# Feed-forward weights staged slice by slice in one kept tile, and a sixth token-group of seven-product down projections, in a fused attention and GEGLU block

## The chip, the cores and the metric

The kernel runs on one core of a Trainium2 chip. Its time is device microseconds (us) of one launch. Before the change three runs took 998.12, 999.64 and 999.91 us, a median of 999.64 us. The engines are named as in the profile: PE is the matmul engine and PEld its weight loads, DVE is VectorE, ACT is ScalarE, POOL is GpSimd, and SP issues most of the DMAs.

## The reference

One pre-layernorm transformer block over 2048 tokens of width 640, in float32:

```
h  = x + softmax_windowed(q k^T * 20^-0.5) v @ wo      with q, k, v = layernorm(x) @ wqkv
h2 = h + (gelu(n @ w_gate) * (n @ w_up)) @ w_down      with n = layernorm(h)
```

There are 32 heads of 20 columns; each token sees itself and the 255 before it. The feed-forward part has 1536 inner columns and gelu in its tanh form. Layernorm has no learned scale.

## The kernel before, in words

**Precision.** A float32 matrix is split into two float16 parts, a high part and a low part (the rest after rounding). A product of two such matrices takes three float16 matmuls: high by high, high by low, low by high.

**Feed-forward work.** The tokens are cut into four chunks of 512 (c = 0 to 3), the inner columns into three groups of 512 (fg = 0 to 2). A pair (c, fg) is a group of work; `ORDER` (line 1132) lists the twelve of them: (0,0) (1,0) (0,1) (0,2) (1,1) (1,2), then chunks 2 and 3. For each group the gate and up projections come first. The first three groups use three plain products (`gate_up`, line 1175). The other nine (`PLAIN` = 3) are done in four `Quad`s each (line 1210), one for each 128 inner columns; a Quad uses sums and differences of the weights (`weight_sums`, line 1602, tile `ws`) and of the tokens (`token_sums`, line 1577, tiles `ts0`, `ts`, `wst`) to need fewer matmuls.

**Down projections.** After a group's four Quads its down projection runs, cut into pieces that are slipped between the steps of the next Quads (`fill`, line 1789). The plain form `down` (line 1343) does, for each of four blocks of 128 tokens and two halves of 320 columns, three products of four matmuls, 96 matmuls of 320 columns, and adds each result into the token tile `ht` with one DVE instruction straight from PSUM (8 for a group). The high-by-high, low-by-high and high-by-low products of two blocks and two halves are twelve matrix products for a pair of blocks. `down7` (line 1432) does the eight correction products among them by a scheme of seven, so eleven products of four matmuls for a pair of blocks, 88 matmuls for a group. It has the 8 additions from PSUM too, and beside them 8 results that ACT copies into four small tiles z (`to_z`, line 1458) and DVE adds to `ht`. It also needs four sums of the weights for each group (`seven_weights`, line 1383: two on POOL, two on DVE) and four sums of the tokens for each pair of blocks (`seven_tokens`, line 1411: two on POOL, two on DVE). `SEVEN` is the list of groups that take this form, `ORDER[FIRST7:-1]`.

**Names in the trace.** All instructions have line 199, so they are read by tile. w4 to w6 are the gate weights of the groups fg = 0 to 2, w7 to w9 the up weights, w10 to w12 the down weights, each with h or l for its part. The tile `ts` written from w10, w11 or w12 holds the weight sums of `down7`; its four z tiles lie in the room of w8l, the token sums in that of w9l. `wst` is the staging tile into which the raw float32 weights are loaded. `rr` and `gelt` take the sums that ACT copies out of a Quad's PSUM bank, `gel` the gated result, `ah` and `al` its two parts.

**Loading of weights.** `load_lane` (line 1641) brings the weights on the SP queue. wo and the first gate and up weights go through a ring of small tiles. The other seven (down 0, then gate, up, down of 1 and of 2) each go as a whole into `wst`: all its slices, of 512 columns five times for gate and up and of 640 columns four times for down, are issued together once the weight before it is `ready`, that is, once all slices of that one have been split. After that DVE takes the largest magnitude of each slice (`scale`, line 390), one small matmul spreads it over the partitions, and the split follows: ACT writes the high part of each slice, then the low part is made, for the first two slices by ACT and POOL and for the others by DVE (`split`, `low`).

**Order.** A planner writes all instructions out in one order. `Clock` (line 54) keeps a modelled time for each engine; each strand of work is a generator (a lane) that yields the engine it wants and the modelled time at which its inputs are there. In every turn the first lane in a list of priorities whose engine is free enough and whose inputs are there is stepped. Once the feed-forward part has the chip to itself, `FFBACK` (line 302) says how far an engine may be ahead for a lane to be let in: 0.75 us for what follows matmuls directly, 0.2 for the norms and the two lanes of sums, 0.1 for `token_sums`. On the chip each engine runs its instructions in that order, and waits by semaphores.

The norm of chunk 2 runs beside the group (1,1), the norm of chunk 3 beside (2,0); `token_sums(2)` is held until the last down weight is split, and takes a new tile with the name `wst`. The strand `seven_weights` starts once four Quads are done and the low parts of w8 and w9 are no longer needed.

Of the kernel before, what the change touches and what calls it, by code (L numbers as in the profile page):

```python
# [22 lines left out]
P = 128  # L23
# [230 lines left out]
def block_kernel(ctx: ExitStack, tc: tile.TileContext, x, wqkv, wo, wg, wu, wd, out):  # L254
# [57 lines left out]
    def need(*reads, slots=(), when=None, eng="tensor"):  # L312

        def f():
            if when and not when() or any(opened[n] >= banks[n] for n in slots):
                return INF
            return max([nc.ready(reads, eng)]
                       + [nc.slot(psums[n], n, banks[n]) for n in slots])
        return f
# [4 lines left out]
    def on(eng, *reads, when=None, after=None):  # L324
        f = need(*reads, when=when, eng=eng)
        if after is not None:
            return (eng,), lambda: max(f(), nc.others(after, eng))
        return (eng,), f
# [25 lines left out]
    class Weight:  # L354
# [5 lines left out]

        def __init__(self, src, shape, col, e=WE):
            self.src, self.shape, self.col, self.e = src, shape, col, e
            self.have = set()
            self.raw = {}

        @property
        def ready(self):
            return len(self.have) == self.shape[0]

        def load(self, room):  # L370
            for i in range(self.shape[0]):
# [16 lines left out]
            pos["used"] += self.sliced  # L388

        def scale(self, lane, tp="tp"):  # L390
            n = self.shape[0]
            am = nc.tile(lnp, [P, 8], F32, "am" + lane, 2 if lane == "0" else 1)
            nc.vector.memset(am[:, n:n + 1], _pow2(-100))
            for i in range(n):
                if self.hl and self.col != C_K:

                    yield on("scalar", self.raw[0, i])
                    nc.scalar.activation(self.hl[0][:, i, :], self.raw[0, i], AF.Abs,
                                         accum_out=am[:, i:i + 1])
                    continue  # L400
                yield on("vector", when=lambda: (0, i) in self.raw)
                yield on("vector", self.raw[0, i])
                nc.vector.tensor_reduce(am[:, i:i + 1], self.raw[0, i], axis=AX.X, op=ALU.max,
                                        apply_absolute_value=True)
                self.done_with()
            yield on("vector", am)
            nc.vector.tensor_reduce(am[:, 7:8], am[:, 0:n + 1], axis=AX.X, op=ALU.max)

            yield on("vector", am)
            nc.vector.tensor_scalar(am[:, 7:8], am[:, 7:8], _pow2(-self.e), None, op0=ALU.mult)  # L410
            hold = SETTLE if ffpools[1] else 0.0
            bound = need(am, slots=[tp])
            yield ("tensor",), lambda: bound() + hold
            t = bank(tp)
            nc.tensor.matmul(t[:, 0:P], am[:, 7:8].to_broadcast([P, P]), ident, start=True,
                             stop=True)
            pc = pw[:, self.col:self.col + 1]
            sc = sw[:, self.col:self.col + 1]
            yield soon("vector", t)
            nc.vector.tensor_reduce(am[:, 6:7], t[:, 0:P], axis=AX.X, op=ALU.max)  # L420
            done(tp)
            yield on("vector", am)
            nc.vector.tensor_scalar(pc.bitcast(I32), am[:, 6:7].bitcast(I32), 0x7F800000, None,
                                    op0=ALU.bitwise_and)
            yield on("vector", pc)
            nc.vector.tensor_scalar(sc.bitcast(I32), pc.bitcast(I32), -1, 0x7F000000,
                                    op0=ALU.mult, op1=ALU.add)
            self.scaled = True
            yield on("vector", pc)
            nc.vector.tensor_scalar(pc, pc, _pow2(self.e), None, op0=ALU.mult)  # L430
            self.known = True
# [6 lines left out]
        def split(self, pool, spread=0):  # L438
            self.room(pool)
            self.begun = True  # L440
            sc = sw[:, self.col:self.col + 1]
            for i in range(self.shape[0]):
                yield on("scalar", when=lambda: (1, i) in self.raw)
                yield on("scalar", sc, self.raw[1, i])
                nc.scalar.activation(self.hl[0][:, i, :], self.raw[1, i], AF.Copy, scale=sc)
                tasks.append(self.low(i, sc, i < spread))

        def low(self, i, sc, spread):
            hi, lo = (t[:, i, :] for t in self.hl)
            w = self.raw[1, i]  # L450
            if spread:
                yield on("scalar", w)
                nc.scalar.activation(w, w, AF.Copy, scale=sc)
                yield on("gpsimd", w)
                nc.gpsimd.tensor_tensor(lo, w, hi, op=ALU.subtract)
            else:
                yield on("vector", hi)
                nc.vector.scalar_tensor_tensor(lo, w, sc, hi, op0=ALU.mult, op1=ALU.subtract)
            self.have.add(i)
            self.done_with()  # L460
# [670 lines left out]
    NCH = S // (CB * P)  # L1131
    ORDER = [(0, 0), (1, 0), (0, 1), (0, 2), (1, 1), (1, 2)]
    ORDER += [(c, fg) for c in range(2, NCH) for fg in range(FG)]
    PLAIN, FIRST7 = 3, 6
    hts, ga = {}, {}
    ffpools = [None, None]

# [434 lines left out]
        if chunk[c] == CB:  # L1572
            side.append((LATE, token_sums(c)))

    TS, sums = {}, {}

    def token_sums(c):
        hh, hl = hT[c]
        h1, h2 = hh[:, :, :CW], hh[:, :, CW:]
        l1, l2 = hl[:, :, :CW], hl[:, :, CW:]  # L1580
        yield on("vector", when=lambda: ffpools[1] and (c < 2 or W["d", FG - 1].ready))
        t = (nc.tile(ffp, [P, KC, 512], F32, "ts" if c else "ts0") if c % 2 or not c else
             nc.tile(ffpools[0], [P, KC, 512], F32, "wst")).bitcast(F16)
        t = t.rearrange("p c (a n) -> p a c n", a=4)
        for ks in (slice(k, k + 1) for k in range(KC)):
            a, b, m, d = (t[:, i, ks] for i in range(4))
            yield on("vector", h1, h2)
            nc.vector.tensor_tensor(a, h2[:, ks], h1[:, ks], op=ALU.subtract)
            yield on("vector", a, l2)
            nc.vector.scalar_tensor_tensor(b, a, -_pow2(-TE), l2[:, ks], op0=ALU.mult, op1=ALU.add)  # L1590
            yield on("vector", b, l1)
            nc.vector.tensor_tensor(d, l1[:, ks], b, op=ALU.subtract)
            yield on("vector", l2, h2)
            nc.vector.scalar_tensor_tensor(m, l2[:, ks], _pow2(TE), h2[:, ks], op0=ALU.mult,
                                           op1=ALU.subtract)
        TS[c] = t
# [44 lines left out]
    def load_lane():  # L1641
        for w in weights[NW:NW + 3]:
            for turn in range(2):
                yield from w.load_slices(turn)
        rest = weights[NW + 3:]
        for i, w in enumerate(rest):
            yield ("sync",), need(when=lambda: ffpools[0] and (i < 1 or rest[i - 1].ready),
                                  eng="sync")
            t = nc.tile(ffpools[0], [P] + w.shape, F32, "wst")
            w.load([t[:, k, :] for k in range(w.shape[0])])  # L1650

    def scale_lane(todo, lane):
        for i in todo:
            w = weights[i]
            before = {2: W["k"]}.get(i)
            yield on("vector", when=lambda: (w.loaded or w.sliced) and (not before or before.scaled)
                     and (i < NW or B[0].maxima == H) and (i <= NW or B[0].scored))
            yield from w.scale(lane, "ra" if i < NW else "tp")
            if i == 0:
                yield on("vector", sw)  # L1660
                nc.vector.tensor_scalar(qs, sw[:, C_Q:C_Q + 1], _pow2(QE), None, op0=ALU.mult)
                pos["qs"] = 1
            if i == 1:
                yield on("vector", when=lambda: W["q"].known)
                qk_scale()
            if i == 2:
                yield on("vector", sw)
                nc.vector.tensor_scalar(vs, sw[:, C_V:C_V + 1], _pow2(VE), None, op0=ALU.mult)
                pos["vs"] = 1
            if i == NW:  # L1670
                yield on("vector", when=lambda: W["v"].known)
                wo_scale()
            if i > NW:
                kind, fg = later[i - NW - 1]
                if kind == "u":
                    ff_scales(fg)
                    pos["ffk", fg] = 1
                if kind == "d":
                    ff_scales_down(fg)
                    w.down = True  # L1680
# [292 lines left out]
```

## Time and profile before

| | |
|---|---|
| median of 3 runs | 999.64 us (998.12 to 999.91) |
| the profiled execution | 998.68 us, of it 997.0 us from the first to the last instruction |
| mean granted clock | 0.998 of full speed |
| busy share of the span | PE 98%, PEld 75%, DVE 79%, ACT 49%, POOL 34% |

"Busy" is the share of the span in which an engine has at least one instruction running. Matmuls overlap one another, so the time of one matmul is longer than the step from one to the next; work on PE is counted here by steps between starts. The window view gives the busy time of each engine in a stretch, the wait view who kept an engine idle, the timeline the single instructions with, in brackets, the idle time ahead of them and the engine and tile that ended it.

### The profile page before, as it was taken

What the parts mean: (1) busy time and instruction counts of PE and PEld (TensorE: products, weight loads), DVE (VectorE), ACT (ScalarE), POOL (GpSimd) and SP (SyncE); (2) the same over time, 40 slices, a digit from 0 to 9 for tenths busy, and PEclk for the clock granted to TensorE, in tenths of its full rate; (3) what the DMA queues carried; (4) which work ended last, traced back from release to release, by engine and by line L of the source; (5) the groups of instructions that cost most, each with busy time, mean ns of one, the idle gap of its engine ahead of it and who ended that gap; (6) DMA issues with size and microseconds to landing.
All of it is one profiled execution on the core that took longest, in us unless ns stands there. A gap on an engine that the chain in (4) does not pass through costs nothing.

```text
span 997.0 us, 35791 instructions
## 1 busy us (share of the span) xinstructions
PE 976.7 (98%) x15326; PEld 746.1 (75%) x15326; DVE 790.4 (79%) x2246; ACT 485.7 (49%) x859; POOL 341.6 (34%) x498
## 2 busy tenths in 40 slices
PE   8998999999999999999999999999999999999998
PEld 7875777777877777777755754688788888888886
DVE  7878998887866776776797796888976887788784
ACT  5515647575555555555576634343223333443431
POOL 7003335464433333333344411253403223233320
PEclk9999999999999999999999999999999999999999
DMA  8658666743622432222304441234353442223211
GB/s 314 141 112 175 154 166 173 169 128 82 128 72 68 97 93 74 76 73 63 134 16 118 98 154 57 98 135 132 116 184 106 146 146 80 80 80 107 81 54 53
DMA packets 129616, 113.01 MB, mean 113 GB/s; under 512 B 85169, under 2 KB 103345, under 8 KB 129457
## 3 DMA queue, kind: packets, MB, share of 16 engines
q1 hardware_dynamic: 117360, 99.97, 35.8%
q10 hardware_dynamic: 12096, 10.75, 3.4%
q8 instruction: 120, 1.97, 0.8%
q14 instruction: 40, 0.32, 0.1%
HBM read 73.73 MB, written 28.84 MB: 103 GB/s over the span
## 4 chain that ended last, share of the span: by engine, by line
PE 83%; DVE 9%; ACT 3%; DMA 2%; issue 1%; POOL 1%; SPq 0%; ACTq 0%; DVEq 0%
PE mm L199 40%; PE ra L199 12%; PE rb L199 12%; PE pv L199 11%; PE tp L199 9%; DVE junk L199 2%; DVE ht L199 1%; ACT pt L199 1%; DVE wsl L199 1%; DMA qT<-mT 1%; DVE gel L199 1%; DMA qT<-in_wqkv_dram 1%; DVE w1l L199 0%; DMA wst<-in_wu_dram 0%; ACT wst L199 0%
## 5 line engine op out<-in xcount | busy, mean ns | idle before, releaser
L199 POOL TENSOR_SCALAR_AFFINE_SELECT pt<-pt 128x512 f32<-128x512 f32 x352 | 175.4, 514 | 276.9 <-ACT pt L199 259.5
L199 DVE CUSTOM_DVE_ANT_0 junk<-rb,band 128x320 bf16<-128x320 f32 x232 | 113.3, 488 | 36.4 <-PE rb L199 31.2
L199 ACT ACTIVATE pt<-ra,esc 128x640 f32<-128x640 f32 (+2 forms) x132 | 100.4, 768 | 83.1 <-PE ra L199 70.6
L199 ACT ACTIVATE pt<-rb,esc 128x640 f32<-128x640 f32 (+2 forms) x124 | 94.1, 766 | 80.5 <-PE rb L199 78.0
L199 DVE CUSTOM_DVE_ANT_0 junk<-ra,band 128x320 bf16<-128x320 f32 x216 | 105.6, 489 | 34.3 <-PE ra L199 29.3
L199 PE MATMUL pv<-pt,v 128*21 128x128 f32 x2880 | 102.9, 275 | 0.3 <-ACT oT L199 0.2
L199 PEld LDWEIGHTS <-ws 128*128 128x128 f16 x720 | 70.7, 98 | 13.5 <-issue 3.2
L199 PEld LDWEIGHTS <-ah 128*128 128x128 f16 x648 | 63.4, 98 | 23.0 <-issue 0.6
L199 PEld LDWEIGHTS <-qT 60*64 60x64 f16 x1280 | 29.7, 104 | 62.6 <-issue 50.7
L199 PEld LDWEIGHTS pv<-pt,v 128*21 128x21 f32 x2880 | 69.0, 100 | 9.8 <-issue 1.1
L199 PEld LDWEIGHTS <-kT 62*64 62x64 f16 x2880 | 64.4, 106 | 10.8 <-issue 5.9
L199 PEld LDWEIGHTS <-gu 128*128 128x128 f16 (+1 forms) x697 | 51.5, 98 | 25.5
L199 DVE SCALAR_TENSOR_TENSOR ht<-mm,ffk,ht 128x320 f32<-128x320 f32 x86 | 46.9, 545 | 14.3 <-PE mm L199 13.0
L199 PE MATMUL mm<-xh,w1h 128*32 128x256 f16 (+1 forms) x344 | 55.9, 273 | 1.2 <-DVE qks L199 1.2
L199 ACT CAST ah<-gel 128x512 f16<-128x512 f32 x48 | 29.6, 617 | 54.4 <-DVE gel L199 52.8
L199 PE MATMUL mm<-xl,w1h 128*32 128x256 f16 (+1 forms) x362 | 56.0, 273 | 0.0
L199 PE MATMUL mm<-xh,w1l 128*32 128x256 f16 (+1 forms) x356 | 55.9, 273 | 0.0
L199 DVE TENSOR_TENSOR al<-gel,ah 128x512 f16<-128x512 f32 x48 | 43.3, 903 | 12.8 <-ACT ah L199 11.9
L199 PE MATMUL mm<-w3h,oh 128*32 128x320 f16 (+1 forms) x373 | 49.7, 299 | 0.6 <-DVE ht L199 0.6
L199 PE MATMUL mm<-w3h,ol 128*32 128x320 f16 (+1 forms) x361 | 49.7, 299 | 0.0
L199 PE MATMUL mm<-w3l,oh 128*32 128x320 f16 (+1 forms) x364 | 49.7, 299 | 0.0
L199 PE MATMUL mm<-xh,w0l 128*32 128x256 f16 (+1 forms) x361 | 49.3, 273 | 0.0
(354 smaller groups left out, 2645.7 us busy)
## 6 DMA issues: line engine op xcount, KB each, us to landing
ws<-wsums SPq DMA_DIRECT2D x24, 640.0 KB
qk<-qks ACTq DMA_DIRECT2D x32, 256.0 KB
wsums<-ws SPq DMA_DIRECT2D x12, 640.0 KB
qT<-qk SPq DMA_DIRECT2D x72, 80.0 KB
kT<-qk SPq DMA_DIRECT2D x72, 80.0 KB
ht<-in_x_dram SPq DMA_DIRECT2D x16, 320.0 KB
h_dram<-ht SPq DMA_DIRECT2D x16, 320.0 KB
ht<-h_dram SPq DMA_DIRECT2D x16, 320.0 KB
```

What stands on the lines that cost most here:

```text
L199: r = real(*args, **kw)
```

## The change

Two things change. First, the seven later weights are no longer loaded as a whole. One `wst` tile is taken once and kept; each weight is loaded in five slices of 512 columns (the down weights too, across their row of 2560), and slice i of a weight is loaded as soon as slice i of the weight before has been split. `scale` may begin when the first slice is on its way. `token_sums(2)` uses the kept tile. Second, `FIRST7` goes from 6 to 5, so that the group (1,2) also takes its down projection by `down7`: six groups in place of five.

```
         def __init__(self, src, shape, col, e=WE):
             self.src, self.shape, self.col, self.e = src, shape, col, e
+            self.n = shape[0]
             self.have = set()
             self.raw = {}
         @property
         def ready(self):
-            return len(self.have) == self.shape[0]
+            return len(self.have) == self.n
+
+        def load_pieces(self, room, prev):
+            self.n = KC
+            src = self.src.rearrange("p a b -> p (a b)")
+            for i in range(KC):
+                yield ("sync",), need(when=lambda: not prev or i in prev.have, eng="sync")
+                self.raw[0, i] = self.raw[1, i] = room[:, i, :]
+                nc.sync.dma_start(room[:, i, :], src[:, i * 512:(i + 1) * 512])
+            self.loaded = True
+
+        def parts(self, i):
+            if self.n == self.shape[0]:
+                return [t[:, i, :] for t in self.hl]
+            return [t.rearrange("p a b -> p (a b)")[:, i * 512:(i + 1) * 512] for t in self.hl]
...
         def scale(self, lane, tp="tp"):
-            n = self.shape[0]
+            n = self.n
...
-            for i in range(self.shape[0]):
+            for i in range(self.n):
                 yield on("scalar", when=lambda: (1, i) in self.raw)
                 yield on("scalar", sc, self.raw[1, i])
-                nc.scalar.activation(self.hl[0][:, i, :], self.raw[1, i], AF.Copy, scale=sc)
+                nc.scalar.activation(self.parts(i)[0], self.raw[1, i], AF.Copy, scale=sc)
                 tasks.append(self.low(i, sc, i < spread))
         def low(self, i, sc, spread):
-            hi, lo = (t[:, i, :] for t in self.hl)
+            hi, lo = self.parts(i)
...
-    PLAIN, FIRST7 = 3, 6
+    PLAIN, FIRST7 = 3, 5
...
-    TS, sums = {}, {}
+    TS, sums, stages = {}, {}, []
...
         t = (nc.tile(ffp, [P, KC, 512], F32, "ts" if c else "ts0") if c % 2 or not c else
-             nc.tile(ffpools[0], [P, KC, 512], F32, "wst")).bitcast(F16)
+             stages[0]).bitcast(F16)
...
         rest = weights[NW + 3:]
-        for i, w in enumerate(rest):
-            yield ("sync",), need(when=lambda: ffpools[0] and (i < 1 or rest[i - 1].ready),
-                                  eng="sync")
-            t = nc.tile(ffpools[0], [P] + w.shape, F32, "wst")
-            w.load([t[:, k, :] for k in range(w.shape[0])])
+        yield ("sync",), need(when=lambda: ffpools[0], eng="sync")
+        stages.append(nc.tile(ffpools[0], [P, KC, 512], F32, "wst"))
+        for prev, w in zip([None] + rest, rest):
+            yield from w.load_pieces(stages[0], prev)
...
-            yield on("vector", when=lambda: (w.loaded or w.sliced) and (not before or before.scaled)
+            yield on("vector", when=lambda: (w.loaded or w.sliced or (0, 0) in w.raw) and (not before or before.scaled)
```

## Rows read from the trace of the kernel before

**Rows 1.** The page: busy time of each engine; the chain that ended last, by engine.
```profile
PE 976.7 (98%) x15326; PEld 746.1 (75%) x15326; DVE 790.4 (79%) x2246; ACT 485.7 (49%) x859; POOL 341.6 (34%) x498
...
PE 83%; DVE 9%; ACT 3%; DMA 2%; issue 1%; POOL 1%; SPq 0%; ACTq 0%; DVEq 0%
```

**Rows 2.** Windows: busy us (instructions) of each engine, TensorE clock, DMA share, GB/s.
```profile
500.00:575.00 75.00, 72.65 (x1374) 47.21 (x1373) 59.95 (x162) 50.36 (x78) 32.87 (x57) 1.00 0.30 73
575.00:645.00 70.00, 69.63 (x372) 36.50 (x371) 57.13 (x147) 28.34 (x43) 11.60 (x10) 1.00 0.31 104
645.00:680.00 35.00, 34.08 (x291) 28.21 (x289) 30.91 (x51) 13.42 (x27) 17.71 (x12) 1.00 0.31 118
...
705.00:770.00 65.00, 62.81 (x523) 51.70 (x522) 50.72 (x103) 20.11 (x45) 14.73 (x10) 0.97 0.41 134
770.00:805.00 35.00, 35.00 (x299) 28.97 (x297) 29.37 (x73) 10.36 (x23) 7.94 (x6) 1.00 0.45 138
...
841.00:877.00 36.00, 36.00 (x310) 30.17 (x309) 29.72 (x47) 14.47 (x32) 10.31 (x6) 1.00 0.21 74
```

**Rows 3.** Waits of PE from 575 to 770: us in total, times, longest.
```profile
PE tp L199 <- ACT rr L199: 2.2, 1, 2.2
PE tp L199 <- DVE am L199: 0.5, 1, 0.5
PE ra L199 <- ACT rs L199: 0.4, 1, 0.4
PE mm L199 <- DVE ht L199: 0.4, 1, 0.4
```

**Rows 4.** Timeline of POOL, DVE and ACT from 703.7 to 709: start, us, instruction.
```profile
703.81 1.39 POOL L199 TENSOR_TENSOR ws<-w5h,ws 128x640 f16<-128x640 f16 x1 [0.94 <-DVE lyai L199]
703.83 1.39 DVE L199 TENSOR_TENSOR lyi<-lyi,lyai 128x1 f32<-128x1 f32 x1
705.16 2.60 POOL L199 TENSOR_TENSOR ts<-w10l 128x1280 f16<-128x1280 f16 x1
...
705.25 2.85 DVE L199 TENSOR_SCALAR wsl<-wsl,lmvi,lyi 128x640 f32<-128x640 f32 x1
...
708.18 0.72 ACT L199 CAST wsl<-wsl 128x640 f16<-128x640 f32 x1 [6.59 <-DVE wsl L199]
...
708.82 0.36 ACT L199 COPY rr<-tp 128x256 f32<-128x256 f32 x1
```

**Rows 5.** Timeline of PE from 709 to 714.
```profile
709.23 0.99 PE L199 MATMUL tp<-h1l,ws 128*128 128x256 f16 x5 [2.19 <-ACT rr L199]
...
713.08 0.71 PE L199 MATMUL rb<-h1h,w5h 128*128 128x256 f16 x5
713.62 0.71 PE L199 MATMUL rb<-h1l,w5h 128*128 128x256 f16 x5
```

**Rows 6.** Timeline of the SP queue: the load of the last weight through `wst`.
```profile
645.50 1.76 SPq L199 DMA_DIRECT2D wst<-in_wd_dram  x4
```

**Rows 7.** Timeline of PE: the first twelve matmuls of (1,2)'s down projection, and the next.
```profile
770.85 0.30 PE L199 MATMUL mm<-w12h,ah 128*128 128x320 f16 x1
...
772.48 0.71 PE L199 MATMUL ra<-h0h,gu 128*128 128x256 f16 x5
```

**Rows 8.** Groups of DVE, 770 to 980: instructions | busy us, mean ns | idle before.
```profile
L199 DVE TENSOR_TENSOR ht<-ht,w8l 128x320 f32<-128x320 f32 x40 | 30.4, 779 | 4.3 <-ACT w8l L199 4.3
...
L199 DVE SCALAR_TENSOR_TENSOR w9l<-w9l,al 128x512 f16<-128x512 f16 x10 | 12.9, 1293 | 3.8 <-POOL w9l L199 3.8
...
L199 DVE SCALAR_TENSOR_TENSOR w9l<-al,ah 128x512 f16<-128x512 f16 x10 | 6.8, 682 | 0.4 <-PE mm L199 0.4
...
L199 DVE SCALAR_TENSOR_TENSOR ts<-ts,w11h 128x1280 f16<-128x1280 f16 x2 | 3.0, 1481 | 0.0
```

**Rows 9.** Timelines of ACT and of PE about 785, beside the norm of chunk 3.
```profile
784.71 0.37 ACT L199 COPY rr<-tp 128x256 f32<-128x256 f32 x1
...
785.13 0.71 PE L199 MATMUL tp<-h0l,ws 128*128 128x256 f16 x5
```

## The prediction

> **What bounds the kernel now.** I read the page first. PE is busy for 976.7 of the 997.0 us, and 83% of the chain that ended last is its own work, against 9% for DVE [rows 1]. So a change pays only where it takes matmuls away or closes a gap on PE. The windows say where gaps are [rows 2]: 2.35 us of idle time from 500 to 575 (the end of the attention, with the first feed-forward group in it), 0.37 from 575 to 645, 0.92 from 645 to 680, 2.19 from 705 to 770, and nothing from 770 to 805 and from 841 to 877. In the wait view the gaps from 575 to 770 have four causes [rows 3]: one wait of 2.2 us for ACT's copy `rr`, and three of 0.4 to 0.5 us.
>
> The timeline shows where the 2.2 us come from. Two POOL instructions, of 1.39 and of 2.60 us, follow each other from 703.81 to 707.76. Beside the first, a DVE instruction of one column per partition takes 1.39 us. Beside the second, the last scaling of a norm takes 2.85 us. ACT's cast of that row block waits 6.59 us for it, and the copy `rr`, which PE needs, stands behind the cast in ACT's queue [rows 4]. PE stands still for 2.19 us and then starts at half the pace: four sets of five matmuls take 3.85 us from 709.23 to 713.08, while the next set takes 0.54 [rows 5]. At that pace four take 2.16, so 1.69 us go to the clock after the wait; the granted clock of 705 to 770 is 0.97 [rows 2]. Price of such a stall: 2.19 + 1.69 = 3.88 us.
>
> **The seventh group form for (1,2).** Its down projection starts at 770.85, and twelve matmuls take 1.63 us to 772.48 [rows 7], 0.136 us each. `down7` needs 88 in place of 96, so 8 x 0.136 = 1.09 us of PE go. PE has no idle time there, so all of it counts.
>
> What it adds on DVE, by [rows 8]: 8 additions of z at 0.779 us (6.2), four token sums, two at 1.293 and two at 0.682 (4.0), and two weight sums at 1.48 (3.0), together 13.2 us. The eight additions from PSUM are in both forms. The weight sums of the first group of the list still come at 705, now for w12 in place of w10; those for (2,0) move into the last visits of (1,2). The stretch from 770 to 805 has 35 - 29.37 = 5.63 us of idle DVE time [rows 2]. So 7.6 us don't fit. They have somewhere to go: norm and token sums of chunk 3 are there too, which PE doesn't read for another two groups, and the planner lets them in only when DVE is nearly idle. From 841 to 877, with `down7` in full and DVE busy for 29.72 of 36 us, PE has no idle time [rows 2]. POOL gets 10.31 us, its whole work in such a stretch, beside 7.94; ACT gets eight short copies and is busy for 10.36 of 35 us. Both have room.
>
> What the crowding costs PE the trace can't show, since no stretch has `down7` and a norm together. The lower bound is nothing (841 to 877). The upper is two stalls of the kind at 709, 7.76. There is a sign of thin margin: at 785, beside the norm of chunk 3, ACT's `rr` copy ends at 785.08 and PE goes on at 785.13 [rows 9]; nothing is in hand there, and what comes later on DVE comes later on PE. I take 0.8 us, a fifth of one stall, nearer to the row that shows the form running without a gap.
>
> [...]
>
> **The loading by slices.** Seven weights are loaded through `wst`; three of them, the down weights, have five slices in place of four. That is 35 DMAs in place of 32 on SP, and for each down weight one more reduction, one more high part and one more low part, of 512 in place of 640 columns, over the same 2560 columns in all. Only the fixed cost of some nine short instructions is added, beside 12.9 us of idle DVE time from 575 to 645 [rows 2]: nothing on PE. SP's new waits, one for each slice, stand ahead of its other transfers (blocks of h, results of `ws`); a late low part would hold those back. No wait of PE from 575 to 770 is for a transfer [rows 3], so I count nothing, with one wait of 0.5 us, the size of the short ones there, as the upper end.
>
> What it brings: a weight's slices are in place while the one before is still being split, so the last load, issued at 645.50 [rows 6], and the three weights before it come earlier by a load each, and scaling and splitting move out of 645 to 680, where DVE is busy for 30.91 of 35 us, into 575 to 645, where it is for 57.13 of 70. PE doesn't wait for a weight itself. The three short waits of [rows 3], 1.3 us, lie in that crowd: for the scale of a weight (`am`), for DVE's `ht`, for ACT's `rs`. Bounds: 0 (they come back where the work goes) and -1.3. I take half, -0.65.
>
> The stall at 709 I leave as it is. Both of its parents are tied to PE's own progress: the norm of chunk 2 is let through when the group (0,2) is done, and the long POOL instruction follows the eighth weight sum. Neither waits for a weight, so both meet again unless the plan shifts by a microsecond or two.
>
> **Sum.** -1.09 + 0.8 - 0.65 = -0.94 us. On the profiled execution's 998.68 (997.0 of span and 1.7 around it) that is 997.7. The median of the runs is 0.96 us higher, so I forecast 998.7, no change that can be measured: 0.2%, or 2.0 us, is about what a measurement of this kernel can tell from none.
>
> **Rivals.**
> The stall at 709 goes, and nothing replaces it: -3.88 more, 994.8. For it: it needs two lanes to meet within a microsecond, and every instruction after the first of these loads is planned anew. Against: the two parents above.
>
> DVE is late from 770 to 805: the added 13.2 us meet POOL's 10.31, a norm's instruction is held up as at 705, `rr` stands behind its cast, and PE waits. One such stall in place of my 0.8 gives 998.7 - 0.8 + 3.88 = 1001.8, two give 1005.7. It decides from the point at which less than 7.6 us of the chunk's norm and sums is pushed past 805. For it: 95 to 100% of DVE there, and the margin at 785 [rows 9]. Against: DVE at 83% beside `down7` without a gap [rows 2].
>
> The loading does not do what it says, and only shuffles the end of the attention: weights are read earlier by DVE between 500 and 575, where it already has 59.95 of 75 us and PE 2.35 us of gaps [rows 2]. If these double, 998.7 + 2.35 = 1001.1.
>
> **Chances.** The forecast 0.40, with a range of its own from 996.5 to 1001 (0.09 of it beyond 0.2% on the fast side); the stall gone 0.28; DVE late 0.24 (0.02 of it within 0.2%); the end of the attention 0.08 (0.03 slower). Faster: 0.28 + 0.09 = 0.37. Slower: 0.22 + 0.03 = 0.25. Same: 0.38. The range reaches past the one stall gone and past one new one, 993.8 to 1003.5; left out are two new stalls and a stall gone with gains beside it, under 0.2.
>
> **What would show it.** Right: the down matmuls of (1,2) fall to 88, its first z copies stand near 770, the seventh weight's last slice is loaded well before 645, the waits `am` and `ht` of PE between 640 and 680 are gone, and the gap near 709 stands. Wrong: no gap near 709, or one of over 1 us between 770 and 810 with the cast of a norm ahead of `rr` on ACT; PE busy time that falls by much more or less than 1.1 us; a wait of PE for a transfer or a weight between 575 and 680.

## The result, and the profile after

The changed kernel takes 1002.76 us (median of 8 runs) against 998.98 us for the kernel before on the same chip: a ratio of 1.0035, 95% interval 1.0023 to 1.0047. It is slower, by some 3.5 us. The profiled execution spans 1001.8 us, against 997.0.

The windows after, in the columns of [rows 2]; for 805 to 841, which is not there, the row of before stands first:

```profile
805.00:841.00 36.00, 36.00 (x311) 30.17 (x309) 27.73 (x44) 14.36 (x32) 10.43 (x6) 1.00 0.36 120
...
500.00:575.00 75.00, 74.50 (x1413) 49.05 (x1406) 61.96 (x169) 49.51 (x78) 33.19 (x59) 1.00 0.39 94
575.00:645.00 70.00, 69.17 (x365) 35.85 (x363) 59.88 (x148) 29.36 (x45) 14.19 (x12) 1.00 0.35 114
645.00:680.00 35.00, 35.00 (x304) 29.49 (x302) 25.99 (x55) 14.26 (x32) 14.78 (x12) 1.00 0.19 77
705.00:770.00 65.00, 62.82 (x523) 51.96 (x523) 49.77 (x105) 20.64 (x46) 13.64 (x9) 0.97 0.43 133
770.00:805.00 35.00, 31.33 (x255) 25.55 (x253) 32.23 (x57) 13.49 (x30) 16.02 (x11) 0.95 0.37 118
805.00:841.00 36.00, 33.76 (x287) 27.91 (x286) 33.36 (x66) 13.03 (x29) 8.98 (x6) 1.00 0.37 129
841.00:877.00 36.00, 36.00 (x310) 30.14 (x309) 29.76 (x48) 14.48 (x32) 10.31 (x6) 1.00 0.21 74
```

Three things are to be seen. From 500 to 680 PE has 1.33 us of idle time, where [rows 2] had 3.64: the loading pays. From 705 to 770 the gap and the clock are as before: the stall at 709 stays. And from 770 to 841, where PE never paused, there are now 5.91 us of idle time, and a granted clock of 0.95 in the first half. POOL's work from 770 to 805 has doubled, from 7.94 to 16.02 us.

The wait view of PE from 700 to 900 (us in total, times, longest) names who kept it waiting. One of the two waits for `rr` is that of 709, the other is new, and so are those for `rs`:

```profile
PE tp L199 <- ACT rr L199: 5.9, 2, 3.7
PE ra L199 <- DVE rs L199: 2.2, 2, 1.6
```

The timeline of POOL, DVE, ACT and PE of the kernel after shows how the new stall comes about (start, us, instruction, and in brackets the idle time ahead of it and what ended it):

```profile
769.94 0.82 DVE L199 SCALAR_TENSOR_TENSOR ws<-ws,gu 128x640 f16<-128x640 f16 x1
...
773.33 1.60 POOL L199 TENSOR_TENSOR w9l<-ah 128x512 f16<-128x512 f16 x1
773.84 1.63 DVE L199 SCALAR_TENSOR_TENSOR gel<-rs,ffk,gel 128x512 f32<-128x512 f32 x1
...
776.14 1.45 POOL L199 TENSOR_TENSOR ws<-gu 128x640 f16<-128x640 f16 x1
776.25 1.88 DVE L199 SCALAR_TENSOR_TENSOR w9l<-al,ah 128x512 f16<-128x512 f16 x1
...
778.28 1.48 POOL L199 TENSOR_TENSOR w9l<-w9l,ah 128x512 f16<-128x512 f16 x1 [0.69 <-DVE w9l L199]
778.99 1.11 DVE L199 TENSOR_TENSOR ht<-ht,w8l 128x320 f32<-128x320 f32 x1
...
783.66 1.16 POOL L199 TENSOR_TENSOR w9l<-ah 128x512 f16<-128x512 f16 x1
784.11 1.06 DVE L199 TENSOR_SCALAR wsl<-wsl,lmvh,lyh 128x640 f32<-128x640 f32 x1
785.20 0.72 ACT L199 CAST wsl<-wsl 128x640 f16<-128x640 f32 x1 [4.96 <-DVE wsl L199]
785.83 0.37 ACT L199 COPY rr<-tp 128x256 f32<-128x256 f32 x1
786.25 0.71 PE L199 MATMUL tp<-h0l,ws 128*128 128x256 f16 x5 [3.67 <-ACT rr L199]
786.79 1.16 PE L199 MATMUL tp<-h0h,gu 128*128 128x256 f16 x5
...
790.64 0.71 PE L199 MATMUL rb<-h0l,gu 128*128 128x256 f16 x5
...
807.80 0.70 PE L199 MATMUL ra<-h0h,w5l 128*128 128x256 f16 x5 [0.65 <-DVE rs L199]
...
818.28 0.71 PE L199 MATMUL ra<-h0h,w5l 128*128 128x256 f16 x5 [1.59 <-DVE rs L199]
```

It is the pattern of [rows 4] and [rows 5] again, 80 us later. Each DVE row stands beside a POOL row and is stretched: `gel` takes 1.63 us, where the same form at 786.42 takes 0.74; `w9l` takes 1.88 where [rows 8] has 0.68; the scaling of the norm takes 1.06. ACT's cast waits for the scaling, `rr` stands behind the cast, PE waits 3.67 us, and the next four sets of five matmuls take 3.85 us (786.79 to 790.64) where four take 2.16 at the full pace: 1.69 us for the clock, as at 709. With the two waits for `rs`, 0.65 and 1.59 us, where POOL's weight and token sums of (2,0) lie beside DVE, that is 7.6 us.

### The profile page after: what moved, and what is told of

Same layout as the page of the kernel before. It is cut to its first block, busy times and chain, and to the rows that moved or that the text cites. A ratio compares the mean times of both kernels' runs of the same rounds, so it can differ in the third digit from the quotient of the medians.

```text
span 1001.8 us, 35828 instructions
## 1 busy us (share of the span) xinstructions
PE 978.4 (98%) x15318; PEld 746.8 (75%) x15318; DVE 801.5 (80%) x2266; ACT 490.2 (49%) x870; POOL 350.6 (35%) x504
## 4 chain that ended last, share of the span: by engine, by line
PE 81%; DVE 12%; ACT 3%; DMA 2%; issue 1%; POOL 0%; SPq 0%; ACTq 0%; DVEq 0%
PE mm L199 38%; PE rb L199 12%; PE ra L199 12%; PE pv L199 11%; PE tp L199 8%; DVE ts L199 2%; DVE junk L199 2%; DVE ht L199 1%; DVE am L199 1%; DVE gel L199 1%; ACT pt L199 1%; DMA wsl<-in_wu_dram 1%; DVE w9l L199 0%; DVE wsl L199 0%; DMA wsl<-h_dram 0%
## 5 line engine op out<-in xcount | busy, mean ns | idle before, releaser
L199 PEld LDWEIGHTS <-ah 128*128 128x128 f16 (+1 forms) x636 | 61.1, 98 | 22.6 <-issue 1.0
L199 ACT ACTIVATE gel<-gel,ffk 128x512 f32<-128x512 f32 x36 | 26.0, 723 | 55.1 <-DVE gel L199 54.5
```

The lines of the kernel that those rows point to most:

```text
L199: r = real(*args, **kw)
```

## The experiments

"Six" in a label means six groups with seven products, as in the kernel after; "late" means a later place of ACT's cast, below. All ratios are to the kernel before on the same chip, with their 95% intervals; 0.001 is 1.0 us.

**The two halves of the change, each alone.** `load_only` is the kernel after with `FIRST7 = 6`; `seven_only` is the kernel before with

```diff
-    PLAIN, FIRST7 = 3, 6
+    PLAIN, FIRST7 = 3, 5
```

> The new loading, with five groups of seven products as before. Theory (the sixth group costs the time, beside the norm of chunk 3; the loading gains what PE was ahead of the kernel before at 709, 2.06 us): the gap at 709 stays, no gap from 770 to 841, about 2 us faster than before, 997. Rival (the earlier loads shift DVE's work so that it collides later, whatever the form of the down projection): the gaps after 770 are there too, about 5 us slower than before, 1004.

> The old loading, with six groups of seven products. Theory: the loss is all here: the two new gaps of PE with their slow clock (3.67 + 1.7 and 2.24 us) less 1.1 of matmuls, about 6 us slower than before, 1005. Rival (the loading is what makes the collision): no gaps after 770, 1.1 us faster, 998.

Measured: `load_only` 997.49 us, 0.9968 (0.9957 to 0.9979); `seven_only` 1008.02 us, 1.0072 (1.0058 to 1.0086). So the loading wins 3.2 us and the seven-product form for (1,2) costs 7.2, and their sum, +4.0, is the whole change's +3.5 within its interval. `load_only` has no wait of PE from 770 to 841; `seven_only` has one of 3.67 us for `rr`, as the kernel after.

**The place of ACT's cast.** Where the planner takes the cast of a norm's row block to be ready 3 us later, it places it behind `rr` in ACT's queue:

```diff
-        yield on("scalar", src, when=lambda: not opened[key] and (not when or when()))
+        ready = need(src, when=lambda: not opened[key] and (not when or when()), eng="scalar")
+        late = 3.0 if ffpools[1] and not dst else 0.0
+        yield ("scalar",), lambda: ready() + late
```

> The changed kernel, with ACT's cast of a norm in the feed-forward part planned 3 us after its input, so that it stands behind the copy rr in ACT's queue. Theory (what costs is the place of the cast: DVE's lateness reaches PE through ACT's queue): both waits of PE for rr go, at 707 and at 786, with the slow clock after each, -3.9 and -5.4; the 2.2 us of waits for rs stay: about 993.5. Rival (DVE just has too much to do there): PE waits for DVE itself instead, at rs, gel or ht, and the time stays within 2 us of the changed kernel's 1002.8.

> The new loading with five groups, and the late cast. Theory: the gain of the loading and the gap at 709 gone: 2 + 3.9 us faster than before, 993. Rival (the lateness of DVE comes through in another way): the gap at 709 is replaced by a wait for DVE, 996 to 997.

> The kernel before with one change: the planner believes ACT's cast of a norm's row block ready 3 us later than it does, so the cast is placed later in ACT's queue, behind the copy rr. Nothing is left out. Theory (the 709 stall is the cast's place in ACT's in-order queue): the wait of 2.19 us for rr and the slow pace behind it (1.69 us) go, 3.9 us less than the kernel before, ratio about 0.996. Rival (DVE itself is late there, so rr's own inputs would be late, as at 785 in the kernel after with this edit): a wait of PE for DVE of 1 to 2 us comes in its place and at most 2 us are won.

Measured: `six_cast_late` 1000.25 us, 1.0002 (0.9991 to 1.0013); `load_cast_late` 993.52 us, 0.9937 (0.9923 to 0.9951); `before_cast_late` 997.30 us, 0.9966 (0.9954 to 0.9977). At 709 the planner moved more than the cast. On DVE the norm's scaling now comes ahead of the last weight sum `ws`, and so no longer lies beside POOL's long subtraction. It takes 0.61 us and is done 1.77 us before `rr` starts, as `before_cast_late` shows:

```profile
704.80 0.61 DVE L199 TENSOR_SCALAR wsl<-wsl,lmvi,lyi 128x640 f32<-128x640 f32 x1
705.32 0.82 DVE L199 SCALAR_TENSOR_TENSOR ws<-ws,w8h 128x640 f16<-128x640 f16 x1
...
707.18 0.37 ACT L199 COPY rr<-tp 128x256 f32<-128x256 f32 x1 [3.11 <-PE tp L199]
707.45 0.73 ACT L199 CAST wsl<-wsl 128x640 f16<-128x640 f32 x1
708.10 3.06 POOL L199 TENSOR_TENSOR ts<-w10l 128x1280 f16<-128x1280 f16 x1
```

So the 3.4 us are what the kernel before gains with the stall at 709 gone, close to the 3.88 that the prediction gave it. What the place of the cast alone is worth there is not shown.

At 785 the cast does move alone: in `six_cast_late` DVE's order up to there is that of the kernel after. No wait for `rr` is left, but PE now waits for DVE itself, as the waits from 700 to 900 show. The longest is 2.49 us in place of 3.67, with the slow pace behind it as before, and the time lies between the two forecasts.

```profile
PE ra L199 <- DVE rs L199: 3.6, 3, 2.5
PE ra L199 <- ACT rs L199: 1.3, 1, 1.3
```

So at 785 the queue of ACT added 1.2 us of wait to what DVE was late by; the rest is DVE's own. By its ratio `load_cast_late` is the fastest kernel of the study, faster than both the kernel before and the kernel after.

**Is DVE late because POOL holds it up, or because it has too much to do?** Two kernels keep the order of the kernel after on every engine and run some instructions on one column only:

```diff
-                nc.gpsimd.tensor_tensor(s2, s1, h1, op=ALU.subtract)
+                x, y, z = short("gpsimd", s2, s1, h1) if g < 2 else (s2, s1, h1)
+                nc.gpsimd.tensor_tensor(x, y, z, op=ALU.subtract)
```

and in the same way `s3`, and for (2,0) `t1` and `t3`; in the other kernel DVE's eight `o + z`. `short` gives the first column of each operand, and leaves the planned time as it was.

> The kernel after, with six kinds of POOL instructions run on one column only though they are planned as if in full: the token sums s2 and s3 of (1,2) and (2,0) and the weight sums t1 and t3 of (2,0). The rest of these sums is left out; the order on every engine stays. DVE's work is the whole of it. Theory (DVE is held up by POOL beside it): the durations of DVE from 770 to 785 and at 796, 803 and 814 fall back to their usual ones, the waits of 3.67, 0.65 and 1.59 us and 1.7 us of slow clock go: 5 to 7.6 us less than the kernel after, 995 to 998. Rival (the 13.2 us added on DVE don't fit, POOL beside them or not): the waits stay within 1 us of theirs, 1001 to 1003.

> The kernel after, with DVE's eight additions of z in group (1,2) run on one column only though planned in full (the rest of these additions is left out; the order on every engine stays). POOL's work is the whole of it. DVE loses 8 x 0.7 = 5.6 us, of which some three additions lie ahead of 785. Theory (DVE is held up by POOL beside it): the stretched rows stay stretched; the wait at 786 shrinks only by what the additions ahead of it took, from 3.67 to about 1.5 us, and those at 808 and 818 by less: about 999 to 1000.5. Rival (it is the sum of DVE's work): with 5.6 of the 7.6 us that don't fit gone, the waits go almost wholly, 995 to 997.

Measured: `six_short_pool` 997.57 us, 0.9977 (0.9963 to 0.9990), 5.8 us less than the kernel after by the ratios; `six_short_z` 1002.10 us, 1.0010 (0.9992 to 1.0028), 2.5 less. The timeline of `six_short_pool` has most of DVE's same instructions at their usual durations, and beside the stall at 709 one wait left:

```profile
770.21 0.82 DVE L201 SCALAR_TENSOR_TENSOR ws<-ws,gu 128x640 f16<-128x640 f16 x1
...
774.37 0.75 DVE L201 SCALAR_TENSOR_TENSOR gel<-rs,ffk,gel 128x512 f32<-128x512 f32 x1
...
775.88 0.69 DVE L201 SCALAR_TENSOR_TENSOR w9l<-al,ah 128x512 f16<-128x512 f16 x1
775.90 2.52 POOL L201 TENSOR_TENSOR ws<-gu 128x640 f16<-128x640 f16 x1
...
777.42 1.35 DVE L201 TENSOR_TENSOR ht<-ht,w8l 128x320 f32<-128x320 f32 x1
...
782.78 0.59 DVE L201 TENSOR_SCALAR wsl<-wsl,lmvh,lyh 128x640 f32<-128x640 f32 x1
...
784.45 0.71 PE L201 MATMUL tp<-h0l,ws 128*128 128x256 f16 x5 [1.60 <-ACT rr L201]
```

3.67 became 1.60 us, the clock stayed up (1.00 from 770 to 805), and the waits of 0.65 and 1.59 us went. In the profile that is 2.07 + 1.69 + 2.24 = 6.0 us, near the 5.8 of the timed runs. In `six_short_z` the wait is still 2.76 us and the clock 0.95:

```profile
770.40 0.82 DVE L201 SCALAR_TENSOR_TENSOR ws<-ws,gu 128x640 f16<-128x640 f16 x1
...
783.66 1.06 DVE L201 TENSOR_SCALAR wsl<-wsl,lmvh,lyh 128x640 f32<-128x640 f32 x1
...
785.80 0.71 PE L201 MATMUL tp<-h0l,ws 128*128 128x256 f16 x5 [2.76 <-ACT rr L201]
```

The wait follows DVE one for one. From the start of that `ws` to the end of the scaling DVE needs 15.23 us in the kernel after, 14.32 in `six_short_z` and 13.16 in `six_short_pool`; the waits are 3.67, 2.76 and 1.60. DVE has no idle time in this stretch that the timelines show, so in `six_short_pool` it is the shorter DVE rows that count, and not POOL's results being there earlier.

`six_short_z` is no strong test, and both of its forecasts missed: an addition that stands alone takes 0.48 us, and still 0.14 on one column, so the eight give back 2.6 us of DVE's busy time (798.9 for 801.5 on the pages), not 5.6. `six_short_pool` gives back 8.4 (793.1) with not one DVE instruction less. So most of the cost is DVE being held up. The 1.60 us that remain are not split further: POOL's other additions still stretch a row (`ht` above, 1.35 us), and DVE's queue is longer.

The other way about, with all the work done: `s2` and `s3` of every seven-product group on DVE (`nc.gpsimd` to `nc.vector` in two lines, `on("gpsimd", ...)` with them).

> The kernel after with the token sums s2 and s3 of all seven-product groups on DVE in place of POOL; nothing is left out. It trades 5.2 us of POOL in each group, which hold DVE up, for some 2.7 us of DVE (4 at 0.68 us). Theory (being held up costs about what POOL's instruction lasts): the wait at 786 shrinks from 3.67 to 2 to 3 us and the one at 818 goes; 999 to 1001. Rival (it is the sum of DVE's own work): DVE has still less room, the waits grow by 1 to 3 us; 1003 to 1006.

> The same with the later place of ACT's cast. Nothing is left out. Theory: against the kernel after with the later cast alone (ratio 1.0002), the waits for DVE at 784 (2.49 us) and 815 (0.83 us) shrink to about 1 us together; ratio 0.996 to 0.998. Rival: they grow, 1.001 or more. Neither expects it under the loading with the later cast and no seventh group form (0.9937).

Measured: `six_dve_sums` 1000.26 us, 1.0003 (0.9992 to 1.0014); `six_dve_sums_late` 995.94 us, 0.9955 (0.9942 to 0.9969). DVE has 24 instructions more and is busy for less, 797.2 us in place of 801.5, and the kernel is 3.2 us faster than the one after. The wait at 786 did not shrink to 2 or 3 us as expected: the order changed as well, it is gone, and two others of 1.78 and 1.33 us stand at 794 and 796, for `rs`, behind an addition that takes 2.89 us beside POOL's long subtraction. `six_dve_sums_late` is about where the theory had it, though its waits for `rs` still come to 2.4 us and not to 1. It is not ahead of `load_cast_late` (0.9937, the intervals overlap), which has the plain form for (1,2): no gain is shown here from 88 matmuls in place of 96 beside a norm.

**The stall at 709.** One instruction more on DVE, behind the norm's scaling, keeps POOL's long subtraction from starting beside it:

```diff
+            if g == 0:
+                yield on("vector", when=lambda: pos["quads"] >= FT + 1)
+                nc.vector.memset(t1[:, 0, 0:1], 0.0)
             yield on("gpsimd", dl, when=free(6))
             nc.gpsimd.tensor_tensor(t1, d2, d1, op=ALU.subtract)
```

> The kernel before with one instruction more: DVE clears one column of the tile that POOL's long weight subtraction (2.60 us, at 705.16) writes; the clear stands behind the norm's scaling on DVE, so POOL has to start behind it. All else stands in the same order on every engine, and nothing is left out. Theory (DVE is held up by POOL's instruction beside it): the scaling takes 0.5 to 1 us in place of 2.85, ACT's cast comes some 2 us earlier, the wait for rr falls under 0.4 us and the clock stays up: 3 to 4 us less than before, ratio 0.996 to 0.997. Rival (the scaling is long by itself): it stays at 2.85, the wait stays at 2.2, and the time is that of the kernel before or up to 1 us more, as POOL's result comes later.

Measured: 999.43 us, 0.9995 (0.9980 to 1.0010). The timeline says why the time hardly moved (this execution was 2.95 us later already at the first of these rows, ahead of the edit: 706.78 for 703.83 in [rows 4]):

```profile
706.78 1.39 DVE L199 TENSOR_TENSOR lyi<-lyi,lyai 128x1 f32<-128x1 f32 x1
708.21 0.61 DVE L199 TENSOR_SCALAR wsl<-wsl,lmvi,lyi 128x640 f32<-128x640 f32 x1
...
709.72 3.15 POOL L199 TENSOR_TENSOR ts<-w10l 128x1280 f16<-128x1280 f16 x1 [1.56 <-DVE ts L199]
710.32 3.23 DVE L199 TENSOR_TENSOR wsl<-wsl 128x640 f16<-128x640 f32 x1
...
716.09 2.60 POOL L199 TENSOR_TENSOR ts<-ts,w10l 128x1280 f16<-128x1280 f16 x1 [3.23 <-DVE ts L199]
716.27 3.78 DVE L199 SCALAR_TENSOR_TENSOR ts<-ts,w10h 128x1280 f16<-128x1280 f16 x1
722.09 0.71 PE L199 MATMUL ra<-h1h,w6l 128*128 128x256 f16 x5 [1.62 <-DVE rs L199]
```

The kernel before has two of these DVE instructions as follows:

```profile
709.60 0.82 DVE L199 TENSOR_TENSOR wsl<-wsl 128x640 f16<-128x640 f32 x1
...
713.17 3.78 DVE L199 SCALAR_TENSOR_TENSOR ts<-ts,w10h 128x1280 f16<-128x1280 f16 x1
```

The scaling falls from 2.85 to 0.61 us with nothing changed but POOL's start, and the wait for `rr` goes. But POOL's first subtraction now holds up the next instruction, `wsl<-wsl`, which takes 3.23 us in place of 0.82: DVE wins 2.24 us and loses 2.41. The 3.78 us beside POOL's second subtraction are in both kernels. So DVE is as far along as before, PE comes earlier, and waits 1.62 us for it. From the first row to the end the kernel saves 2.15 us in the profile (0.8 us more of span, less 2.95), about what 2.19 + 1.69 - 1.62 = 2.26 gives; of that the timed runs show 0.5, with 2.0 at the edge of their interval. The mechanism is as expected, the price is not: a long POOL instruction among DVE's has to fall somewhere.

**What the loading wins.** Two kernels on the base of `load_cast_late`. In the first a slice is loaded once the whole weight ahead is split, as the planner sees it; in the second each weight also gets a new staging tile:

```diff
-                yield ("sync",), need(when=lambda: not prev or i in prev.have, eng="sync")
+                yield ("sync",), need(when=lambda: not prev or prev.ready, eng="sync")
```

```diff
-             stages[0]).bitcast(F16)
+             nc.tile(ffpools[0], [P, KC, 512], F32, "wst")).bitcast(F16)
...
-        yield ("sync",), need(when=lambda: ffpools[0], eng="sync")
-        stages.append(nc.tile(ffpools[0], [P, KC, 512], F32, "wst"))
-        for prev, w in zip([None] + rest, rest):
-            yield from w.load_pieces(stages[0], prev)
+        for i, w in enumerate(rest):
+            yield ("sync",), need(when=lambda: ffpools[0] and (i < 1 or rest[i - 1].ready),
+                                  eng="sync")
+            yield from w.load_pieces(nc.tile(ffpools[0], [P, KC, 512], F32, "wst"), None)
```

> The loading of the change alone with the later place of ACT's cast (as in the fastest version so far), but each slice is loaded only when the whole weight ahead of it has been split, as in the kernel before; the kept tile and the five slices stay. Nothing is left out. Theory (what the loading wins is that slices arrive while the weight ahead is still being split): the gain over the kernel before with the cast alone (ratio 0.9966 against 0.9937, 2.9 us) goes; ratio 0.996 to 0.997, and the last down weight is loaded at 645 again. Rival (the kept tile or the five even slices win it): ratio stays at 0.993 to 0.995.

> As the run before it that loads a slice when the whole weight ahead is split, but each weight now gets a new staging tile as in the kernel before, so that on the chip too its first slice waits for the last reader of the weight ahead (with the kept tile, slices still went out one by one as theirs came free: 4.30 us from the first to the last of a weight at 587.93). The five even slices stay. Nothing is left out. Theory (loading beside the splitting wins it): a weight's five loads go out together again, some 17 to 19 us from weight to weight, the last at 640 or later, ratio 0.996 to 0.997, that of the kernel before with the cast alone. Rival (the even slices win it): 0.993 to 0.995.

Measured: `load_whole_late` 994.94 us, 0.9946 (0.9931 to 0.9960); `load_fresh_late` 1001.72 us, 1.0013 (1.0001 to 1.0026). By its numbers the first went to the rival, but it did not do what it was built for. In the SP queue (time of the first of a weight's loads, us from first to last) of `load_whole_late`:

```profile
587.93 4.30 SPq L199 DMA_DIRECT2D wst<-in_wd_dram  x5
...
630.93 3.98 SPq L199 DMA_DIRECT2D wst<-in_wd_dram  x5
```

The planner's condition sets only the order of the queue. With a kept tile each slice waits on the chip for the readers of its own part, so loads still go out one by one, and the last is where it was in `load_cast_late` (629.01) but for 2 us. `load_fresh_late` has them together, each weight 17 to 19 us behind the one ahead:

```profile
599.88 2.43 SPq L199 DMA_DIRECT2D wst<-in_wd_dram  x5
...
654.03 2.23 SPq L199 DMA_DIRECT2D wst<-in_wd_dram  x5
```

That costs 6.7 us against `load_whole_late`, more than expected. The sums `ws` of a weight that was loaded and split late come after PE asks for them (waits of 2.19 and 1.39 us at 655 and 657), and from 645 to 680 PE has 3.99 us of gaps and a clock of 0.95. From 500 to 575, too, it has 3.53 us of gaps at a clock of 0.98, for 1.24 at 1.00 in `load_whole_late`. So the gain hangs on the kept tile, and the even slices alone win nothing: with new tiles they are 4.7 us slower than `before_cast_late`, which loads in the old way. That the gain comes from loading beside the splitting is what the load times suggest; it is not shown alone, since with new tiles the last load is also later (654.03) than in the kernel before (645.50).

## Why the prediction was wrong

The forecast was no change, 998.7 us, and the kernel is slower. The likeliest case failed at one step, the crowding from 770 to 805; what came instead is the rival "DVE is late".

- **The matmuls, -1.09:** right in the count. The page after has 15318 matmuls, eight fewer than [rows 1]; the time they save can't be read apart.
- **The crowding, +0.8: the step that failed.** It measures 7.6 us in the profile, and 7.2 + 1.1 = 8.3 by `seven_only`. That is about the upper bound of the prediction (7.76), not a fifth of one stall. I chose by the row from 841 to 877, where `down7` runs without a gap, and counted busy time: what doesn't fit has somewhere to go. But in that stretch no norm runs; the row that had both, POOL and a norm, was [rows 4], and it had a stall. The planner gave each instruction its usual duration, so it placed DVE's norm and POOL's token sums side by side, and behind them the cast just ahead of `rr`. The margin of nothing at 785 [rows 9] was noted as a sign and priced at next to nothing. The 13.2 us added on DVE were also misread as plain work: the means of [rows 8] hold such stretched rows already, 0.779 us for an addition that takes 0.48 alone and 1.293 for a sum that takes 0.68. Most of what DVE is late by comes from the rows that meet POOL's (`six_short_pool`).
- **Being held up.** The scaling takes 2.85 or 0.61 us by nothing but POOL's start (`before_t1_held`), and POOL's sums on one column take 5.8 us off the kernel. The Trainium skill ("SBUF — State Buffer", section "Who interferes with whom") has DVE and POOL share a port pair: a DVE instruction with two SBUF inputs contends with a POOL instruction that reads SBUF, and issue order decides which of them is blocked. The traces agree: in the kernel after `gel` and `w9l<-al,ah` start 0.51 and 0.11 us behind a POOL row, and each ends 0.54 us after it; in `six_short_pool` the same `w9l` starts 0.02 us ahead of POOL's `ws` and takes 0.69 us, and the POOL row takes 2.52 in place of 1.45.
- **The loading, -0.65: right in sign, five times too small.** `load_only` gives -3.2 (-4.3 to -2.1), beyond my bound of -1.3. I bounded it by the three short waits from 575 to 770 and looked on 500 to 575 only as a risk. Of the 2.31 us of idle time that went from 500 to 680, 1.85 went there, at the end of the attention. The weight loads were early as foreseen (the seventh from 629.01, for 645.50 in [rows 6]), and the added waits on SP cost nothing that shows.
- **The stall at 709, unchanged: right.** It stands at 707.18, 2.21 us long with the same slow pace behind it. Its price of 3.88 us was right too: without it the kernel before is 3.4 us faster. But 1.69 us of it, the slow pace, is not in every execution (last section).

Had the crowding been taken at its upper bound, the sum would be -1.09 + 7.6 - 0.65 = +5.9; with the loading at its measured -3.2 it is +3.3, and +3.5 was measured. The rival with one new stall, 1001.8, lies near the measured 1002.76 by luck: the crowding cost about twice that stall, and the loading took most of the difference back.

## What to carry to other kernels

Judge a crowded stretch by what runs at the same moment on DVE and POOL, not by the busy time of each: a stretch without gaps is no evidence for one that adds a norm beside POOL's work. Where one engine's queue carries both a side lane's work and a copy that PE needs, the side lane's instruction belongs behind the copy when its input may be late; at 785 that took 1.2 us off a wait of 3.67, and the rest stayed. When an edit is made in a planner, look at what else it moved: the later cast also moved the scaling that was held up. A staging tile that is kept lets each slice be overwritten when its own readers are done, and it is the tile, not the order in the queue, that decides it.

## What was not expected of the hardware

A DVE instruction of one value per partition (`lyi`) takes 1.39 us beside a POOL addition of 1.40 us, and 0.15 us with POOL idle (`six_short_pool`, at 789.74). Being held up goes both ways: POOL's long subtraction, 2.60 us in [rows 4], takes 3.15 in `before_t1_held`, where DVE's `gel` (709.65, 0.75 us) had started 0.07 us ahead of it, and then the DVE instruction behind `gel` takes 3.23.

How long PE waits does not settle what the wait costs after it. Behind 2.19 us (709) and 3.67 us (786) the matmuls run at half the pace for four sets of five, 1.69 us more. Behind 2.20 us at the same place in `six_dve_sums` they run on at the full pace, and the clock from 705 to 770 is 1.00:

```profile
708.59 0.71 PE L199 MATMUL tp<-h1l,ws 128*128 128x256 f16 x5 [2.20 <-ACT rr L199]
709.13 0.71 PE L199 MATMUL tp<-h1h,w5h 128*128 128x256 f16 x5
709.68 0.71 PE L199 MATMUL ra<-h1h,w5l 128*128 128x256 f16 x5
```

Behind two waits of 1.78 and 1.33 us, 2 us apart, the same execution falls to half the pace (clock 0.95 from 770 to 805); behind a single wait of 1.60 us in `six_short_pool`, of 1.62 in `before_t1_held` or of 1.92 in `seven_only` (823.05) the pace stays. What decides it these runs do not show.
